# An attention and mixture-of-experts kernel: all float32 products of a tile in four 64x64 quadrants, the first expert's weights loaded from tile 12 on

## The chip, the cores and the metric

The kernel runs on one core of one Trainium2 chip. The metric is the device time in microseconds (us) of one execution, as a median of several runs. A core has TensorE (PE, with its weight loads, PEld, as a row of their own), VectorE (DVE), ScalarE (ACT), GpSimd (POOL) and the queue that issues most DMAs (SP). Line numbers (L239) are those of the kernel before, unless the text says otherwise.

## What is computed

Chunked attention, without a mask, over 4,608 tokens (8 batches of 576, in chunks of 64), and then a layer of experts on its output, in which each token goes to one expert or none:

```python
scores = scale * np.matmul(q_c, k_c.transpose(0, 1, 2, 4, 3))   # chunks of 64, D = 64
scores = scores - np.max(scores, axis=-1, keepdims=True)
attn = np.exp(scores)
attn = attn / (np.sum(attn, axis=-1, keepdims=True) + 1e-09)
x = np.matmul(attn, v_c)          # -> 4608 tokens of 512
...
skip_score = x @ w_skip           # only tokens with skip_score > 0 go on
logits = xc @ w_gate              # 8 experts
e_idx = np.argmax(logits, axis=1)
...
    h = np.maximum(xc[mask] @ w1[e], 0.0)          # 512 -> 1024
    y[mask] = gate_w[mask, None] * (h @ w2[e])     # 1024 -> 512
out[do_compute] = xc + y
```

## The kernel before

**Two parts.** The first part works on 36 tiles of 128 tokens (two chunks of 64, all 8 heads) in float32 and writes the attention's output to `out`. The second gathers the tokens of each expert in blocks of up to 128 rows and runs them through the two layers with float16 pairs (a high and a low part). Between the two, a routing step over groups of 4 to 6 tiles works out for each token its expert and its row.

**A tile's products on TensorE.** Five groups of matmuls belong to each tile, and each float32 matmul stands in the trace as two weight loads and two matmuls, each float32 transpose as one of each:
- `pe_scores` (L232 to L240): q times k, 16 products of 64x64 by 64x64, in four quadrants of the array (two halves of the rows, two of the columns), into a two-bank PSUM tile `sc`; 32 loads and 32 matmuls.
- `pe_ptrans` (L262): four transposes of 128x128 into one PSUM bank, of the pool `ps_s` with two buffers; 4 and 4. `ac_pt` (L269) copies the result to SBUF on ACT.
- `pe_pv` (L274): the attention times v, 16 products in quadrants, into `xq`, two banks; 32 and 32.
- `pe_logit` (L307): the product with `w_skip` and `w_gate`, four accumulating matmuls of 128x128 by 128x9, into spare columns of the `xq` of a later tile; 8 and 8. `ve_logit` (L315) copies the 9 columns out on DVE.
- `pe_xt` (L295): four transposes of 128x128 of the attention's output into the other `ps_s` buffer; 4 and 4. `ac_xt` (L302) copies it out on ACT.

Between them stand `ac_scores` (L242), `ve_max` (L247, the row maximum on DVE and the subtraction on POOL), `ac_exp` (L257) and `ve_x` (L285, the division on DVE, and the DMA of the tile to `out` on SP).

**The order is written out by hand.** The loop at L636 runs steps i = 0 to 41; step i issues the scores of tile i, the first transpose of tile i-2, the product with v of tile i-3, the logits of tile i-5 and the second transpose of tile i-4, in that order on TensorE. On each engine and on SP the work runs in the order in which the loop issues it. The q and k of a pair of tiles are loaded (L130) four pairs ahead, with five buffers; the v of a pair likewise. In the last six steps, in which no new tile begins, parts of the first expert's first layer (`l1_steps`, L487, with PSUM banks of `ps_s`) are put between (`DRAIN`).

**The first expert's weights.** `W_LOAD` lists the eight steps in which a pair of weight chunks of 512 KB is loaded (`load_pair`, L349, four buffers), `W_CONV` eight steps in which one of the sixteen halves is converted, the high part on ACT (L359) and the low part on DVE (L360). The eight halves that are left are converted after the loop (L760). In steps 32 and 38 POOL gathers the first blocks of the second part from `out` (`gather_at`, L652), ahead of the step's `ve_max` in POOL's order.

**PSUM** has eight banks here: `rk` one, `ps_s` two, `dbank` one, `sc` two, `xq` two. After the loop the first part's pools are closed and `bpool` and `ps_h` take their room (L691 to L694).

## Time and profile before

| | |
|---|---|
| median of three runs | 391.61 us (391.16 to 392.31) |
| the profiled execution | 391.34 us, of which the span from the first to the last instruction is 389.5 us |
| mean granted TensorE clock over the span | 0.944 |
| tile 0 to tile 33 begun on TensorE | 5.3 to 130.5 us |
| last logits of the first part | about 165 us |
| second part | from there to the end |

The profile gives busy time by engine, groups of instructions by line, a timeline by engine, the chain of waits that ended last, the DMA queues with their packets, and sums by stretches of time. In a timeline, what stands in square brackets at a row's end is the idle time of the engine ahead of it and what ended it; "issue" is time in which the engine waited for nothing that the profile shows. In the rows of stretches, x and a number is the count of instructions that began in the stretch.

### The profile page before, as it was taken

The page shows a single profiled execution, that of the slowest core. Times are in us where ns is not written, and L with a number is a line of the kernel's source. Part 1 is how long each engine was busy: PE and PEld are TensorE (multiplying, and loading weights), DVE is VectorE, ACT ScalarE, POOL GpSimd, SP SyncE. Part 2 cuts the span into 40 slices and gives each one's busy share as a digit, 9 for nine tenths or more (in the row PEclk, how much of TensorE's full clock was granted, in tenths as well). Part 3 has the DMA queues.
Part 4 walks back from the last instruction along what each step waited for, and adds up shares of the span by engine and source line. Part 5 has one row for each costly group of instructions (what it writes and reads, how often), then busy time and mean ns, then how long its engine had stood idle before and what let it go on. Part 6 is the DMA issues. An engine that isn't in the chain of part 4 may idle for free.

```text
span 389.5 us, 11031 instructions
## 1 busy us (share of the span) xinstructions
PE 359.6 (92%) x4472; PEld 256.1 (66%) x4472; DVE 248.3 (64%) x580; ACT 185.8 (48%) x319; POOL 125.5 (32%) x151
## 2 busy tenths in 40 slices
PE   6989899999999799867988999999999999999992
PEld 3667788888788588843575554475574766758470
DVE  2444447796577548477976776677696767966520
ACT  2665537676566454260152554455365444645220
POOL 4332217363353724212171411421513335111000
PEclk9899659999899979996998999999999999999998
DMA  7999979999862311200763676577756876655000
GB/s 262 415 404 412 408 282 306 332 337 371 313 248 82 111 56 56 82 0 0 259 197 134 215 237 232 164 262 223 255 183 187 276 230 217 206 186 183 27 24 26
DMA packets 26792, 81.81 MB, mean 210 GB/s; under 512 B 3335, under 2 KB 3336, under 8 KB 26738
## 3 DMA queue, kind: packets, MB, share of 16 engines
q1 hardware_dynamic: 23634, 71.74, 53.7%
q0 software_dynamic: 3104, 9.33, 6.5%
q8 instruction: 37, 0.61, 0.6%
q14 instruction: 17, 0.14, 0.1%
HBM read 67.20 MB, written 14.35 MB: 209 GB/s over the span
## 4 chain that ended last, share of the span: by engine, by line
PE 79%; DVE 6%; issue 6%; DMA 3%; POOL 2%; ACT 1%; SPq 0%; POOLq 0%; DVEq 0%
PE sp L516 23%; PE hp L494 19%; PE xq L312 9%; PE xq L282 6%; PE sc L239 6%; PE sp L266 5%; PE sp L299 4%; PE sp L494 2%; PE xt L479 2%; DMA xg<-out,recsi 2%; DVE wset L360 2%; DMA st<-in_qk 1%; PE rk L158 1%; PE rk L449 1%; DVE x L524 1%
## 5 line engine op out<-in xcount | busy, mean ns | idle before, releaser
L516 PE MATMUL sp<-wset,ht 128*128 128x512 f16 (+2 forms) x528 | 107.4, 387 | 0.0
L494 PEld LDWEIGHTS <-wset 128*128 128x128 f16 x864 | 79.8, 98 | 21.4 <-issue 3.1
L494 PE MATMUL hp<-xt,wset 128*128 128x288 f16 (+4 forms) x768 | 89.3, 278 | 0.9 <-DVE xt L481 0.6
L516 PEld LDWEIGHTS <-ht 128*128 128x128 f16 (+2 forms) x528 | 45.4, 100 | 50.4 <-issue 6.3
L216 DVE SCALAR_TENSOR_TENSOR wset<-wst,wset 128x1024 f16<-128x1024 f32 x56 | 67.6, 1217 | 9.5 <-ACT wset L215 9.5
L251 POOL TENSOR_TENSOR px<-sc,mx 128x512 f32<-128x512 f32 x36 | 39.0, 1085 | 87.2 <-DVE mx L249 85.8
L219 POOL DMA_INDIRECT out<-x,recsi x18 | 24.9, 1382 | 114.5 <-DVE x L524 99.3
L215 ACT ACTIVATE wset<-wst 128x1024 f16<-128x1024 f32 x56 | 57.7, 1048 | 0.0
L498 ACT ACTIVATE ht<-hp 128x288 f16<-128x288 f32 (+4 forms) x64 | 25.2, 393 | 61.1 <-PE hp L494 59.8
L499 DVE SCALAR_TENSOR_TENSOR ht<-hp,ht 128x288 f16<-128x288 f32 (+4 forms) x64 | 27.1, 433 | 23.4 <-ACT ht L498 22.7
L312 PE MATMUL xq<-csb,xc 128*128 128x9 f32 x288 | 41.0, 270 | 0.0
L312 PEld LDWEIGHTS xq<-csb,xc 128*128 128x128 f32 x288 | 37.9, 205 | 2.5
L288 DVE TENSOR_SCALAR rr<-xq 128x8 f32<-128x8 f32 x36 | 5.9, 164 | 49.2 <-PE xq L312 46.4
L480 ACT ACTIVATE xt<-xt 128x512 f16<-128x512 f32 (+2 forms) x20 | 10.6, 528 | 53.1 <-PE xt L479 39.8
L304 ACT ACTIVATE xc<-sp 128x512 f32<-128x512 f32 x36 | 21.4, 594 | 26.7 <-PE sp L299 26.7
L282 PE MATMUL xq<-sv,pz 64*64 64x65 f32 x1152 | 27.7, 234 | 4.1 <-issue 3.5
L239 PE MATMUL sc<-st 64*64 64x64 f32 x1152 | 28.3, 240 | 3.5 <-DMA st<-in_qk 2.2
L259 ACT ACTIVATE px<-px 128x512 f32<-128x512 f32 x36 | 22.6, 628 | 18.5 <-POOL px L251 18.5
L239 PEld LDWEIGHTS sc<-st 64*64 64x64 f32 x1152 | 22.8, 148 | 11.6 <-issue 9.4
L249 DVE TENSOR_REDUCE mx<-sc 128x8 f32<-128x512 f32 x36 | 24.4, 677 | 8.7 <-ACT sc L244 8.7
L282 PEld LDWEIGHTS xq<-sv,pz 64*64 64x64 f32 x1152 | 22.2, 143 | 11.7 <-issue 9.4
L266 PE MATMUL sp<-csb,px 128*128 128x128 f32 x144 | 25.9, 305 | 3.3 <-ACT px L259 2.9
(173 smaller groups left out, 389.0 us busy)
## 6 DMA issues: line engine op xcount, KB each, us to landing
wst<-in_wall SPq DMA_DIRECT2D x64, 512.0 KB, 4.4
st<-in_qk SPq DMA_DIRECT2D x34, 512.0 KB, 7.8
sv<-in_vo SPq DMA_DIRECT2D x18, 520.0 KB, 7.7
out<-xa SPq DMA_DIRECT2D x36, 256.0 KB, 3.5
st<-in_qk SPq DMA_DIRECT2D x4, 256.0 KB, 3.5
xg<-out,recsi POOLq DMA_INDIRECT x18, 5.7
out<-x,recsi POOLq DMA_INDIRECT x18, 5.1
csb<-in_cst SPq DMA_DIRECT2D x1, 266.5 KB, 4.6
```

Of the source, the lines that this page charges most:

```text
L215: nc.scalar.activation(w[:, 0, fc, :], st, AF.Copy, scale=SW)
L216: nc.vector.scalar_tensor_tensor(w[:, 1, fc, :], st, SW, w[:, 0, fc, :], op0=ALU.mult, op1=ALU.subtract)
L219: ins = nc.gpsimd.indirect_dma_start(**kw)
L239: nc.tensor.matmul(sp[halves[c], a, j], st[halves[r], 0, i, w], st[halves[r], 1, i, w], start=(j == 0), stop=True, skip_group_check=True)
L251: nc.gpsimd.tensor_tensor(px, T[t].pop("sc"), mx.unsqueeze(2).to_broadcast([P, H, CH]), op=ALU.subtract)
L266: nc.tensor.transpose(pt[:, j, :], px[:, j].rearrange("p a s -> p (a s)"), ident)
L282: nc.tensor.matmul(xq[w, a, j * (D + 1):(j + 1) * (D + 1)], pz[r, j, w], v[r, c, j], start=(j == 0), stop=True, skip_group_check=True)
L312: nc.tensor.matmul(lg, xc[:, j], C("wsg")[:, j * (NE + 1):(j + 1) * (NE + 1)], start=(j == 0), stop=(j == KC - 1), skip_group_check=True)
L494: nc.tensor.matmul(hp, w()[:, a, fc, j * P:(j + 1) * P], xt[:, b, j, :n], start=(m == 0), stop=(m == 11))
L498: nc.scalar.activation(ht[:, 0, fc, :n], hp, AF.Relu)
L499: nc.vector.scalar_tensor_tensor(ht[:, 1, fc, :n], hp, 0.0, ht[:, 0, fc, :n], op0=ALU.max, op1=ALU.subtract)
L516: nc.tensor.matmul(y[c * P // cg:c * P // cg + n], ht[:, a, fc, o:o + n], w[:, b, fc, P * KC:], start=(f == 0 and m == 0), stop=(f == fw - ...
```

## The change

1. Both transposes are made in quadrants: 16 float32 products of a 64x64 piece with a 64x64 identity in place of four transposes of 128x128, into one two-bank tile `tp`, which has a single buffer and serves both transposes. ACT copies it out from two banks.
2. The logits are 16 products of 64x64 by 64x9, into both banks of `xq`; DVE adds the two banks in place of the copy.
3. `ps_s`, the two-bank pool, is opened only after the tile loop's step 35; its room is that of `sc`, which goes into a pool of its own.
4. `W_LOAD` and `W_CONV` move to later steps.
5. In a step, the early gathers come after `ve_max` in place of ahead of it.
6. `bpool` and `ps_h` are given the option `reuse_waits="tile"`.

```diff
-W_LOAD = (3, 6, 10, 14, 17, 20, 22, 24)
-W_CONV = (7, 10, 12, 13, 15, 18, 19, 22)
+W_LOAD = (12, 14, 16, 18, 21, 25, 29, 33)
+W_CONV = (15, 17, 19, 21, 23, 25, 27, 29)
...
-    ps_s = ctx.enter_context(tc.tile_pool(name="ps_s", bufs=2, space=PSUM))
...
+    scpool = tc.tile_pool(name="ps_c", bufs=1, space=PSUM, side="right")
+    ps_c = scpool.__enter__()
...
+    QUADS = ((0, 0), (1, 1), (0, 1), (1, 0))
...
+    def two_banks(pool, name):
+        return pool.tile([P, 2, DM], F32, name=name)[:, :, :KC * CH].rearrange("p a (j s) -> p a j s", j=KC)
+
+    def by_quads(src):
+        dst = two_banks(ps_p, "tp")
+        for j in range(KC):
+            for r, c in QUADS:
+                nc.tensor.matmul(dst[halves[c], r, j], src[halves[r], j * P + c * CH:j * P + (c + 1) * CH], ident[halves[r], halves[r]], start=(j == 0), stop=True, skip_group_check=True)
+        return dst
+
+    def from_quads(dst, src):
+        nc.scalar.activation(dst.rearrange("p j (r q) -> p r j q", r=2), src, AF.Copy)
...
     def pe_ptrans(t):
-        px = T[t].pop("px")
-        pt = bank().rearrange("p (k q) -> p k q", k=KC)
-        for j in range(KC):
-            nc.tensor.transpose(pt[:, j, :], px[:, j].rearrange("p a s -> p (a s)"), ident)
-        T[t]["pt"] = pt
+        T[t]["pt"] = by_quads(T[t].pop("px"))
...
     def pe_xt(t):
-        x = T[t].pop("x")
-        xp = bank().rearrange("p (k q) -> p k q", k=KC)
-        for j in range(KC):
-            nc.tensor.transpose(xp[:, j, :], x[:, j * P:(j + 1) * P], ident)
-        T[t]["xp"] = xp
+        T[t]["xp"] = by_quads(T[t].pop("x"))
...
     def pe_logit(t):
...
-        lg = xq[:, 0, XW:XW + NE + 1]
+        lg = xq[:, :, XW:XW + NE + 1]
         for j in range(KC):
-            nc.tensor.matmul(lg, xc[:, j], C("wsg")[:, j * (NE + 1):(j + 1) * (NE + 1)], start=(j == 0), stop=(j == KC - 1), skip_group_check=True)
+            for r, c in QUADS:
+                nc.tensor.matmul(lg[halves[c], r], xc[halves[r], j, halves[c]], C("wsg")[halves[r], j * (NE + 1):(j + 1) * (NE + 1)], start=(j == 0), stop=(j == KC - 1), skip_group_check=True)
...
-        nc.vector.tensor_copy(lgs[g][:, i], T[t].pop("lg"))
+        nc.vector.tensor_reduce(lgs[g][:, i], T[t].pop("lg").rearrange("p a n -> p n a"), axis=AX.X, op=ALU.add)
...
-        for m in gather_at.get(i, ()):
-            early_gather(m)
         on(ve_x, i - 4)
         on(ve_logit, i - 6)
         on(ve_max, i - 1)
+        if i == NT:
+            scpool.__exit__(None, None, None)
+            ps_s = ctx.enter_context(tc.tile_pool(name="ps_s", bufs=2, space=PSUM, side="right"))
+        for m in gather_at.get(i, ()):
+            early_gather(m)
...
-    bpool = ctx.enter_context(tc.tile_pool(name="bpool", bufs=3))
-    ps_h = ctx.enter_context(tc.tile_pool(name="ps_h", bufs=3, space=PSUM))
+    bpool = ctx.enter_context(tc.tile_pool(name="bpool", bufs=3, reuse_waits="tile"))
+    ps_h = ctx.enter_context(tc.tile_pool(name="ps_h", bufs=3, space=PSUM, reuse_waits="tile"))
```

More of the change, by code (lines that the diff above doesn't have):

```diff
@@ L230, in fill @@
             budget -= c
+    def two_banks(pool, name):
[8 more added lines that the diff above has]
+        nc.scalar.activation(dst.rearrange("p j (r q) -> p r j q", r=2), src, AF.Copy)
     def pe_scores(t):
         st, i = T[t].pop("st"), t % TP
-        sp = ps_p.tile([P, 2, DM], F32, name="sc")[:, :, :KC * CH].rearrange("p a (j s) -> p a j s", j=KC)
+        sp = two_banks(ps_c, "sc")
         for j in range(KC):
-            for k in range(4):
-                a, r, c = k // 2, k % 2, (k + k // 2) % 2
+            for r, c in QUADS:
+                a = r ^ c
                 w = slice((2 * j + a) * CH, (2 * j + a + 1) * CH)
@@ L259, in ac_exp @@
         nc.scalar.activation(px, px, AF.Exp, scale=1.0 / math.sqrt(D))
-        T[t]["px"] = px.rearrange("p (j a) s -> p j a s", a=2)
+        T[t]["px"] = px.rearrange("p h s -> p (h s)")
     def pe_ptrans(t):
-        px = T[t].pop("px")
-        pt = bank().rearrange("p (k q) -> p k q", k=KC)
-        for j in range(KC):
-            nc.tensor.transpose(pt[:, j, :], px[:, j].rearrange("p a s -> p (a s)"), ident)
-        T[t]["pt"] = pt
+        T[t]["pt"] = by_quads(T[t].pop("px"))
     def ac_pt(t):
         pz = ap.tile([P, KC, P], F32, name="pz", bufs=2)
-        nc.scalar.activation(pz, T[t].pop("pt"), AF.Copy)
+        from_quads(pz, T[t].pop("pt"))
         T[t]["pz"] = pz
@@ L278, in pe_pv @@
         for j in range(KC):
-            for k in range(4):
-                a, c = k % 2, (k + k // 2) % 2
+            for a, c in QUADS:
                 r, w = halves[a], halves[c]
@@ L295, in pe_xt @@
     def pe_xt(t):
-        x = T[t].pop("x")
-        xp = bank().rearrange("p (k q) -> p k q", k=KC)
-        for j in range(KC):
-            nc.tensor.transpose(xp[:, j, :], x[:, j * P:(j + 1) * P], ident)
-        T[t]["xp"] = xp
+        T[t]["xp"] = by_quads(T[t].pop("x"))
     def ac_xt(t):
         xc = ap.tile([P, KC, P], F32, name="xc", bufs=2)
-        nc.scalar.activation(xc, T[t].pop("xp"), AF.Copy)
+        from_quads(xc, T[t].pop("xp"))
         T[t]["xc"] = xc
@@ L309, in pe_logit @@
         xq = T[t + 2]["xq"] if t + 2 < NT else ps_p.tile([P, 2, DM], F32, name="xq")
-        lg = xq[:, 0, XW:XW + NE + 1]
+        lg = xq[:, :, XW:XW + NE + 1]
         for j in range(KC):
-            nc.tensor.matmul(lg, xc[:, j], C("wsg")[:, j * (NE + 1):(j + 1) * (NE + 1)], start=(j == 0), stop=(j == KC - 1), skip_group_check=True)
+            for r, c in QUADS:
+                nc.tensor.matmul(lg[halves[c], r], xc[halves[r], j, halves[c]], C("wsg")[halves[r], j * (NE + 1):(j + 1) * (NE + 1)], start=(j == 0), stop=(j == KC - 1), skip_group_check=True)
         T[t]["lg"] = lg
```

## The prediction

> **What bounds the kernel now.** I read the page's head, then the first part in stretches, then TensorE's timeline in a quiet tile and in a disturbed one, then the DMA packets around the disturbed ones. The page says how many instructions TensorE gets, and that a DMA queue of its own carries instructions:

> ```profile
> span 389.5 us, 11031 instructions
> PE 359.6 (92%) x4472; PEld 256.1 (66%) x4472; DVE 248.3 (64%) x580; ACT 185.8 (48%) x319; POOL 125.5 (32%) x151
> ...
> q8 instruction: 37, 0.61, 0.6%
> L239 PE MATMUL sc<-st 64*64 64x64 f32 x1152 | 28.3, 240 | 3.5 <-DMA st<-in_qk 2.2 <-issue 1.3
> L266 PE MATMUL sp<-csb,px 128*128 128x128 f32 x144 | 25.9, 305 | 3.3 <-ACT px L259 2.9 <-issue 0.3
> L312 PE MATMUL xq<-csb,xc 128*128 128x9 f32 x288 | 41.0, 270 | 0.0
> ```

> 0.61 MB in 37 packets is 16 KB each. The groups are from the view of lines with shapes kept apart: over 36 tiles, 1152 is 32 matmuls per tile for the scores, 144 is 4 for a transpose, 288 is 8 for the logits. The first part in stretches (columns: length; busy us and instructions of PE, PEld, DVE, ACT, POOL; granted clock; DMA share; GB/s):

> ```profile
> 8.20:23.00 14.80, 13.77 (x305) 9.57 (x305) 6.86 (x19) 9.08 (x16) 4.53 (x5) 0.88 1.03 413
> 23.00:42.50 19.50, 16.24 (x385) 13.64 (x385) 7.89 (x22) 12.34 (x21) 5.58 (x5) 1.00 1.03 408
> 42.50:59.50 17.00, 17.00 (x227) 14.31 (x231) 8.63 (x27) 6.59 (x13) 3.37 (x4) 0.50 0.87 329
> 59.50:97.10 37.60, 37.32 (x898) 32.17 (x891) 28.01 (x87) 26.79 (x50) 18.99 (x30) 1.00 0.95 337
> 97.10:131.20 34.10, 32.94 (x744) 27.96 (x743) 23.91 (x88) 19.93 (x36) 14.85 (x28) 0.95 0.53 196
> 131.20:165.40 34.20, 29.86 (x448) 25.86 (x449) 18.70 (x74) 14.84 (x29) 13.79 (x27) 0.90 0.24 79
> ```

> TensorE is busy nearly throughout, except at 23 to 42.5, where the DMA engines are full. A quiet tile, then TensorE's disturbed places:

> ```profile
> 61.45 0.69 PE L239 MATMUL sc<-st 64*64 64x64 f32 x32
> 62.07 0.66 PE L266 MATMUL sp<-csb,px 128*128 128x128 f32 x4
> 62.66 0.70 PE L282 MATMUL xq<-sv,pz 64*64 64x65 f32 x32
> 63.28 1.06 PE L312 MATMUL xq<-csb,xc 128*128 128x9 f32 x8
> 64.20 0.64 PE L299 MATMUL sp<-csb,xa 128*128 128x128 f32 x4
> 64.76 0.69 PE L239 MATMUL sc<-st 64*64 64x64 f32 x32
> ```

> ```profile
> 21.98 0.34 PE L239 MATMUL sc<-st 64*64 64x64 f32 x6
> 23.03 0.68 PE L239 MATMUL sc<-st 64*64 64x64 f32 x26 [0.72 <-issue]
> ...
> 29.39 0.46 PE L282 MATMUL xq<-sv,pz 64*64 64x65 f32 x16 [1.38 <-issue]
> ...
> 35.68 0.45 PE L239 MATMUL sc<-st 64*64 64x64 f32 x14 [0.55 <-issue]
> ...
> 41.95 0.33 PE L282 MATMUL xq<-sv,pz 64*64 64x65 f32 x4 [1.29 <-issue]
> ...
> 99.09 0.62 PE L282 MATMUL xq<-sv,pz 64*64 64x65 f32 x26 [0.85 <-issue]
> ```

> A quiet tile takes 64.76 - 61.45 = 3.31 us, with no gap: 0.62, 0.59, 0.62, 0.92, 0.56 us from start to start. The disturbed places are the finding. TensorE stops in the middle of a group (after 6 of 32 matmuls), where no data can be missing, and four of these stops end 6.3 us apart. What came between two stops, and what the instruction queue q8 did meanwhile (stretches 23.02 to 29.37 and 29.37 to 35.67; packets of 23.02 to 26.9, 26.9 to 27.0, 103.3 to 103.5 and 106.6 to 106.7):

> ```profile
> 23.02:29.37 6.35, 4.97 (x126) 4.12 (x126) 2.10 (x6) 3.97 (x7) 2.08 (x2) 1.00 1.03 403
> 29.37:35.67 6.30, 5.75 (x126) 4.90 (x127) 3.73 (x11) 3.71 (x7) 1.42 (x1) 1.00 1.03 408
> ```

> ```profile
> q1 hardware_dynamic: 515, 1.57, 102.2%
> ```

> ```profile
> q8 instruction: 1, 0.02, 67.1%
> ```

> ```profile
> q8 instruction: 1, 0.02, 30.1%
> ```

> ```profile
> q8 instruction: 1, 0.02, 55.5%
> ```

> **The change part by part.** *Quadrants in place of transposes and logits.* By durations alone this is a gain. At each change between 128x128 and 64x64 TensorE's loads sit idle:

> ```profile
> 24.22 0.56 PEld L282 LDWEIGHTS xq<-sv,pz 64*64 64x64 f32 x32 [0.17 <-issue]
> ```

> A group of 32 that needs no change of shape should thus take 0.62 - 0.17 = 0.45 us, and five of them 2.25 us in place of 3.31. [...]

> By count it is a loss. Per tile the transposes go from 4 + 4 to 32 + 32 (loads and matmuls), twice, and the logits from 8 + 8 to 32 + 32: 56 + 56 + 48 = 160 more instructions, 320 per tile in place of 160. In 2.25 us that asks for a block each 1.8 us, and none came faster than 3.3. So I expect TensorE to wait for instructions throughout the tile loop, and cost the stretch from 23.0 us to 131.2 (scores of tiles 6 to 33) in blocks. Instructions now, from the rows of stretches: 770 + 458 + 1789 + 1487 = 4504. Added: 27 tiles by 160 = 4320, and 384 that the first tiles add ahead of 23.0 (four and two transposes and one logits group by 56 and 48), which must be fetched too. Together 9208, or 36.0 blocks of 256.

> The price of a block is the unknown. Below: 3.3 us, the shortest seen; 36.0 x 3.3 = 119 us. Above: 6.3 us with full queues; 227 us, but that can't last, since the stretch's 32.9 MB (the rows' lengths by their GB/s) are 80 us of transfers at 412 GB/s, and a slower tile loop leaves the queues emptier. Taking the price as a straight line from 3.3 at a low DMA share to 6.3 at 1.03, the share being 80 us over the stretch, gives 4.7 us and 169 us. I take less, because transfers come in bursts: those of one step (0.26 MB out, and 0.5 or 1 MB in) last 2 to 3 us, and a request that falls into one waits for the rest of it, some 1.2 us, in 58% of cases (80 us over 140). 3.3 + 0.7 = 4.0 us, and 36.0 x 4.0 = 144 us against 108.2 now: +36, with ends of +11 and +61. Nothing hides this: TensorE is the engine that the chain runs through.

> A lower granted clock, as in the row of 0.50, would cost little on top. A group of 32 takes 1.06 us there (the chain of waits):

> ```profile
> 44.81 1.06 PE sc L239 x32
> ```

> Five of them are 5.3 us at most, about the 320/256 x 4.0 = 5.0 us that fetching a tile takes. I count it in the upper end.

> *One buffer `tp` for both transposes.* A transpose now waits until ACT has copied the one before it. In the quiet tile the copy ends 0.77 us after the group behind the transposes began:

> ```profile
> 64.93 0.60 ACT L304 ACTIVATE xc<-sp 128x512 f32<-128x512 f32 x1
> ```

> Behind the first transpose stand two groups, which cover it; behind the second only the scores, 0.45 us, so 0.77 - 0.45 = 0.32 us per tile is left: a tile of 2.25 + 0.32 = 2.6 us, if instructions came. Queued behind the waiting matmul are the product with v and all that follows. Under 5 us of fetching it is covered: zero.

> *Weights later.* The same bytes; three loads of 0.5 MB leave the full stretch before 42.5, others come after; on SP each still stands behind its step's loads of q, k and v and ahead of the tile's output. As tiles are fetch-bound, each load makes some block later wherever it stands: 0, within 4 us either way. The conversions on ACT and DVE lie beside TensorE, and eight halves are left for the end, as now (a group of the lines, and the chain):

> ```profile
> L359 ACT ACTIVATE wset<-wst 128x512 f16<-128x512 f32 x16 | 9.5, 619 | 0.6 <-DMA wst<-in_wall 0.6
> ```

> ```profile
> 177.79 4.90 DVE wset L360 x8
> ```

> *Gathers behind the subtraction.* Now a gather holds POOL ahead of a step's subtraction, which TensorE waits for (the chain of waits):

> ```profile
> 131.26 1.01 POOL xg L219
> ...
> 132.30 1.06 POOL px L251
> ...
> 134.06 0.66 PE sp L266 x4
> ```

> With the order turned round the subtraction goes first; that saves 1 to 3 us of the wait before 134.06, and the gather comes a microsecond later; its reader, the block's transposes, stands two steps on.

> *The last steps.* From 131.2 to 165.4 are 897 instructions; 1056 of the added 5760 are left for it: 1953, 7.6 blocks, at 3.3 us 25 us. That is under the 34.2 us that this stretch takes, which is a chain of waits across engines. So: -3 from the gathers, within -6 and +6, since fetches and waits may add up.

> *The rest* (the reduction on DVE in place of a copy, `reuse_waits`, the pool's later opening) lies beside TensorE: zero, within 2 us either way. The second part's instructions don't change, and fetching doesn't bind there, with 2348 of them in 174 us, a block in 19 us:

> ```profile
> 215.00:389.00 174.00, 166.66 (x1175) 103.93 (x1173) 114.34 (x158) 77.33 (x121) 47.33 (x34) 0.99 0.58 187
> ```

> Sum, on the profiled execution's 391.3 us (span 389.5 and 1.8 around it; the median of the runs is 391.6, the same within 0.1%): 391.3 + 36 - 3 = 424 us. With the ends: 391.3 + 11 - 6 = 396, and 391.3 + 61 + 6 = 458.

> **The rivals.** *Faster: instructions keep up.* If a second block can be on its way while TensorE asks for more, or blocks come faster than 3.3 us when asked faster, the tile falls to the 2.6 us of the buffer `tp`: 27 tiles by 0.7 is -19 (the 80 us of transfers still fit into the 89 that are left), the gathers -3, 369 us. For it: before, in quiet stretches, nobody needed a block sooner than each 5 us, so the least price is never measured under hunger and empty queues at once. Against it: four stops 6.3 us apart, with no packet begun in the 3.9 us after the restart. [...]

> *No change: the price falls to 3.0 us.* At 108.2 / 36.0 = 3.0 us per block the stretch is as long as now. Of that, 2.5 us pass between packet and restart anyway (26.9 to 29.39). Then 391.3 - 3 = 388, or 391 with some loss at the end. It needs the request to reach an idle DMA engine nearly always; with the DMA engines busy for 80 of 108 us that is unlikely.

> *Slower for another reason:* instructions keep up, but the single `tp` and ACT's three copies and one exponential (2.4 us at 0.6 each), with conversions in between, hold a tile above 3.31 us. The point is a copy that ends 0.7 us later than I count; a conversion of 0.62 us ahead of it nearly gets there, in eight tiles: 8 by 0.6 is +5 against the -19. That ends at 374 us and goes with the first rival.

> **How the numbers follow.** Forecast, fetch-bound tile loop, 396 to 458 us: 0.75. Instructions keep up, 365 to 386 us: 0.20. Price near 3.0 us, 386 to 396 us: 0.05. A difference of 0.3%, about 1.2 us, is what a measurement can tell from none. Of the third case nearly all lies outside of that, on both sides. Faster by over 0.3%: 0.22; within 0.3%: 0.03; slower: 0.75. The predicted time is 424. The range takes the forecast's case but for its last tenth (up to 455) and reaches down to 378, which takes in the case near 3.0 and some of the first rival's. The forecast's own range is 396 to 458.

> **What would show it.** Right: some 58 to 60 packets on q8 in place of 37, and 4472 + 2880 = 7352 matmuls; in the tile loop, stops that end on "issue" in the middle of groups, every 256 instructions, 3.3 to 5 us apart; tiles of 4 to 6 us. Groups of 32 at 0.47 us between stops would show the gain from unchanged shapes as real but unused. Wrong: packets on q8 closer than 3 us together, tiles under 3.3 us, TensorE's waits ending on ACT's copy (the single `tp`). Then the first rival holds, and my reading that one block at a time is on its way is the step that failed.

## The result, and the profile after

| | before | after |
|---|---|---|
| median of four runs on one chip | 391.96 us (391.16 to 395.23) | 446.53 us (443.38 to 449.66) |
| the profiled execution | 391.34 us | 447.94 us |
| its span | 389.5 us | 446.1 us |
| mean granted clock | 0.944 | 0.854 |

The ratio is 1.137 (95% interval 1.127 to 1.148): slower, by 55 us. Executions that ran over 1.5% longer than the fastest of their kernel are left out of the ratios here and below, so a ratio need not be that of the medians. The page of after (from its head, slices, queues, the shares of the chain of waits, and the groups):

```profile
span 446.1 us, 16738 instructions
PE 367.9 (82%) x7352; PEld 273.5 (61%) x7352; DVE 250.2 (56%) x580; ACT 185.7 (42%) x319; POOL 125.0 (28%) x151
...
q8 instruction: 59, 0.97, 0.9%
...
PE 73%; issue 16%; DVE 4%; DMA 3%; ACT 1%; POOL 1%; SPq 0%; POOLq 0%; ACTq 0%; DVEq 0%
...
L254 PE MATMUL sc<-st 64*64 64x64 f32 x1152 | 37.0, 269 | 15.4 <-issue 12.9
L241 PE MATMUL tp<-csb,px 64*64 64x64 f32 x1152 | 36.4, 274 | 15.7 <-issue 12.8
```

7352 matmuls and 59 packets of instructions, 22 more than before. TensorE's busy time rose by only 8 us for 64% more matmuls. The time is in the last column: 12.9 and 12.8 us of idle time ahead of the scores and the first transpose end on "issue", and "issue" holds 16% of the chain that ended last, where it held 6% before.

Where the 56.6 us of the two profiled executions come from is read by cutting both at the same events: the scores of tile 6 begun, of tile 33 begun, and the last logits done. Stretches of before, then of after (columns as in the prediction):

```profile
22.00:130.50 108.50, 103.12 (x2214) 87.70 (x2213) 68.75 (x222) 66.25 (x119) 42.33 (x66) 0.91 0.83 307
130.50:165.10 34.60, 30.25 (x479) 26.13 (x479) 19.07 (x74) 14.84 (x29) 14.25 (x28) 0.90 0.24 78
165.10:389.50 224.40, 208.06 (x1444) 130.94 (x1443) 152.69 (x265) 94.11 (x153) 60.67 (x43) 0.97 0.53 170
```

```profile
31.60:190.60 159.00, 113.00 (x4379) 104.95 (x4376) 70.60 (x223) 66.30 (x120) 43.91 (x68) 0.69 0.56 188
190.60:224.00 33.40, 27.40 (x1021) 23.84 (x1013) 19.07 (x72) 14.69 (x28) 12.01 (x26) 0.91 0.25 82
224.00:446.10 222.10, 206.02 (x1453) 130.07 (x1448) 152.67 (x265) 94.11 (x154) 60.80 (x44) 0.98 0.53 172
```

Tiles 6 to 33 take 50.5 us more, the tiles ahead of them 9.6 (31.6 against 22.0), the last steps 1.2 less and the second part 2.3 less; together 56.6. In the long stretch TensorE is busy for 113 of 159 us, where it was for 103 of 108.5, and the DMA engines are emptier, not fuller (0.56 against 0.83). So of the 50.5 us 9.9 are more busy time, at a lower clock, and 40.6 more idle time; by the view of waits 44.1 us of TensorE's idle time there end on "issue", where 4.8 did before. In this stretch the view of the DMA queues lists

```profile
q8 instruction: 34, 0.56, 1.4%
```

so 159.0 / 34 = 4.68 us per block, and 4379 + 4376 = 8755 records are 34.2 blocks of 256. TensorE's timeline shows how a block is lived on:

```profile
81.91 1.01 PE L241 MATMUL tp<-csb,px 64*64 64x64 f32 x25
84.30 0.38 PE L241 MATMUL tp<-csb,px 64*64 64x64 f32 x4 [1.38 <-issue]
...
87.06 0.94 PE L254 MATMUL sc<-st 64*64 64x64 f32 x24
89.40 0.38 PE L254 MATMUL sc<-st 64*64 64x64 f32 x4 [1.40 <-issue]
```

It stops inside a group, once in the first transpose and 5.1 us later in the scores, and each stop is 1.4 us long. Stretches that are cut by turns at a restart of TensorE and at the start of the next q8 packet (78.94 restart, 81.89 packet, 84.30 restart, and so on; a count takes in every instruction that runs in a row, so that one at a border stands in both):

```profile
78.94:81.89 2.95, 2.95 (x103) 2.87 (x102) 1.56 (x5) 1.09 (x2) 1.32 (x8) 0.50 0.90 329
81.89:84.30 2.41, 1.03 (x29) 0.93 (x26) 1.30 (x3) 0.60 (x1) 2.16 (x2) 0.50 0.55 144
84.30:87.20 2.90, 2.90 (x109) 2.90 (x112) 0.66 (x3) 1.12 (x2) 0.65 (x1) 0.50 0.84 336
87.20:89.40 2.20, 0.81 (x31) 0.62 (x24) 1.08 (x3) 0.60 (x1) 1.04 (x1) 0.50 0.50 153
89.40:93.28 3.88, 3.70 (x128) 3.51 (x127) 0.78 (x3) 2.23 (x4) 0.00 (x0) 0.50 0.75 263
93.28:95.50 2.22, 0.00 (x0) 0.00 (x0) 1.55 (x4) 0.00 (x0) 1.19 (x1) 0.50 0.54 137
```

Odd rows run from restart to packet (2.95, 2.90, 3.88 us), even rows from packet to restart (2.41, 2.20, 2.22). The DMA share is 0.75 to 0.90 in the odd rows and 0.50 to 0.55 in the even ones. Each even row holds a stop: TensorE is busy in it for 1.03, 0.81 and 0.00 us. The long stretch is like these rows for the most part: 27 of its 34 packets are followed by a stop of 0.2 us or more, which ends 2.2 to 2.7 us behind the packet's start, 2.37 on average. The other seven blocks came before TensorE had used up the one ahead of them. Between the ends of two stops stand 254 to 256 loads and matmuls, or 510 where one block without a stop lies between. From a restart to the next packet 1.0 to 3.9 us pass, 2.3 on average, at a DMA share of 0.74; from there to the restart the share is 0.43. So I read that one block at most is on its way, and that it is asked for when the one ahead of it has come.

### The profile page after: what moved, and what is told of

The parts are those of the page before. It is cut to its first block, busy times and chain, and to the rows that moved or that the text cites. A ratio compares the mean times of both kernels' runs of the same rounds, so it can differ in the third digit from the quotient of the medians.

```text
span 446.1 us, 16738 instructions
## 1 busy us (share of the span) xinstructions
PE 367.9 (82%) x7352; PEld 273.5 (61%) x7352; DVE 250.2 (56%) x580; ACT 185.7 (42%) x319; POOL 125.0 (28%) x151
## 4 chain that ended last, share of the span: by engine, by line
PE 73%; issue 16%; DVE 4%; DMA 3%; ACT 1%; POOL 1%; SPq 0%; POOLq 0%; ACTq 0%; DVEq 0%
PE sp L523 20%; PE hp L501 16%; PE tp L241 14%; PE xq L292 6%; PE sc L254 5%; PE xq L319 5%; PE sp L501 2%; PE xt L486 2%; DMA xg<-out,recsi 2%; DMA st<-in_qk 1%; ACT xc L245 1%; DVE wset L367 1%; PE rk L456 1%; PE rk L160 1%; DVE x L531 1%
## 5 line engine op out<-in xcount | busy, mean ns | idle before, releaser
L266 POOL TENSOR_TENSOR px<-sc,mx 128x512 f32<-128x512 f32 x36 | 39.0, 1085 | 146.2 <-DVE mx L264 144.0
L254 PE MATMUL sc<-st 64*64 64x64 f32 x1152 | 37.0, 269 | 15.4 <-issue 12.9
L241 PE MATMUL tp<-csb,px 64*64 64x64 f32 x1152 | 36.4, 274 | 15.7 <-issue 12.8
L245 ACT ACTIVATE xc<-tp 128x512 f32<-128x512 f32 x36 | 21.5, 597 | 65.7 <-PE tp L241 65.7
L241 PE MATMUL tp<-csb,xa 64*64 64x64 f32 x1152 | 37.4, 269 | 9.4 <-issue 9.4
L254 PEld LDWEIGHTS sc<-st 64*64 64x64 f32 x1152 | 32.5, 180 | 18.6 <-issue 18.1
L292 PE MATMUL xq<-sv,pz 64*64 64x65 f32 x1152 | 36.9, 270 | 8.3 <-issue 8.3
L319 PE MATMUL xq<-csb,xc 64*64 64x9 f32 x1152 | 33.3, 222 | 10.8 <-issue 10.7
L241 PEld LDWEIGHTS tp<-csb,px 64*64 64x64 f32 x1152 | 29.8, 179 | 19.8 <-issue 14.3
L319 PEld LDWEIGHTS xq<-csb,xc 64*64 64x64 f32 x1152 | 31.9, 177 | 11.9 <-issue 11.8
L292 PEld LDWEIGHTS xq<-sv,pz 64*64 64x64 f32 x1152 | 31.8, 181 | 11.2 <-issue 10.4
L241 PEld LDWEIGHTS tp<-csb,xa 64*64 64x64 f32 x1152 | 31.9, 178 | 10.5 <-issue 10.5
```

Source lines behind the costliest of these rows:

```text
L241: nc.tensor.matmul(dst[halves[c], r, j], src[halves[r], j * P + c * CH:j * P + (c + 1) * CH], ident[halves[r], halves[r]], start=(j == 0), ...
L245: nc.scalar.activation(dst.rearrange("p j (r q) -> p r j q", r=2), src, AF.Copy)
L254: nc.tensor.matmul(sp[halves[c], a, j], st[halves[r], 0, i, w], st[halves[r], 1, i, w], start=(j == 0), stop=True, skip_group_check=True)
L266: nc.gpsimd.tensor_tensor(px, T[t].pop("sc"), mx.unsqueeze(2).to_broadcast([P, H, CH]), op=ALU.subtract)
L292: nc.tensor.matmul(xq[w, a, j * (D + 1):(j + 1) * (D + 1)], pz[r, j, w], v[r, c, j], start=(j == 0), stop=True, skip_group_check=True)
L319: nc.tensor.matmul(lg[halves[c], r], xc[halves[r], j, halves[c]], C("wsg")[halves[r], j * (NE + 1):(j + 1) * (NE + 1)], start=(j == 0), st ...
```

## The experiments

The theory, which I call the fetch theory: the tile loop is bound by the delivery of TensorE's instructions, one block of 256 at a time, and the price of a block depends on what the DMA engines do while it is awaited. Its rivals: the lower clock (0.69 in the long stretch) is what costs the time; the single `tp` makes TensorE wait for ACT; the later weights do. The runs stand beside runs of the kernel before on the same chip, whose medians were 390.67, 389.27 and 391.79 us for the three groups of runs below. In the tables "long stretch" is from the scores of tile 6 to those of tile 33, and packets are those of q8 in it.

### The added instructions, taken back in three steps

`n160` is after with both transposes of 128x128 again, into the first bank of the same single `tp`, and the logits as before; its count of instructions per tile is that of before. In `n208` only the logits stay in quadrants, in `n264` the logits and the first transpose. The edit, for one transpose:

```diff
-        T[t]["xp"] = by_quads(T[t].pop("x"))
+        x = T[t].pop("x")
+        xp = ps_p.tile([P, 2, DM], F32, name="tp")[:, 0].rearrange("p (k q) -> p k q", k=KC)
+        for j in range(KC):
+            nc.tensor.transpose(xp[:, j, :], x[:, j * P:(j + 1) * P], ident)
+        T[t]["xp"] = xp
```

> The changed kernel with both transposes and the logits back in 128x128 (160 instructions per tile on TensorE as before), all else of the change kept: the single buffer tp, the later weights, the gathers behind the subtraction, the option of the later pools. Fetch theory (a block of 256 instructions costs TensorE 4.5 to 4.7 us and the count sets the tile loop): 18 blocks in the stretch of tiles 6 to 33, no more than TensorE's own 3.3 us per tile, so 384 to 396 us in all. Rival, the single tp and ACT's copies hold a tile: the tile loop stays near 5 us per tile, 430 us or more. Rival, the late weight loads cost the time: 430 us or more as well.

> As the one with 160, but the logits stay in quadrants: 208 instructions per tile. Fetch theory: some 23 blocks of 4.5 us, 104 us for the stretch that took 108 before: 385 to 405 us in all, with stops that end on issue in every tile. By durations alone (no fetch bound) it would gain about 0.4 us per tile on the one with 160, 12 us or more. Rival single tp: 430 us or more.

> The changed kernel with only the second transpose back in 128x128: 264 instructions per tile. Fetch theory: some 29.6 blocks of 4.6 us, 136 us for the stretch: 405 to 425 us, on a line with the kernels of 208 and 320 by count. By durations alone it would be slower than the changed kernel, since it brings back two changes of shape per tile. Rival clock (the granted clock of one half in most of the tile loop is the cause, not the fetching): no line by count; 440 us or more as long as the clock stays at one half.

| | instructions per tile | median, us | long stretch, us | packets in it | clock in it | second part, us |
|---|---|---|---|---|---|---|
| before | 160 | 390.67 | 108.5 | 18 | 0.91 | 224.4 |
| `n160` | 160 | 387.98 (381.89 to 390.8) | 110.4 | 18 | 0.92 | 222.4 |
| `n208` | 208 | 399.41 (395.73 to 400.74) | 122.1 | 23 | 0.82 | 222.1 |
| `n264` | 264 | 419.96 (415.7 to 421.99) | 135.3 | 28 | 0.77 | 222.6 |
| after | 320 | 446.53 | 159.0 | 34 | 0.69 | 222.1 |

(The row of before has its median from this chip, and the rest from the profiled execution shown above; the row of after is from the first comparison.) The ratios are 1.027 (1.012 to 1.041) for `n208` and 1.074 (1.057 to 1.090) for `n264`. The long stretch of the three, in this order:

```profile
22.00:132.40 110.40, 103.52 (x2213) 86.93 (x2212) 70.36 (x223) 67.71 (x120) 42.75 (x67) 0.92 0.82 297
```

```profile
23.80:145.90 122.10, 102.74 (x2865) 84.91 (x2864) 70.06 (x222) 66.85 (x120) 45.08 (x69) 0.82 0.76 270
```

```profile
29.80:165.10 135.30, 106.72 (x3618) 93.91 (x3617) 68.47 (x217) 67.33 (x120) 42.06 (x66) 0.77 0.66 221
```

TensorE's busy time stays between 103 and 107 us, while its records go from 4425 to 7235. The length follows the records, which the count of packets mirrors: 122.1 / 23 = 5.3 us per block at a DMA share of 0.76, 135.3 / 28 = 4.8 at 0.66, 159.0 / 34 = 4.7 at 0.56. A stop stands behind 13 of the 23 packets, 18 of the 28 and 27 of the 34; so in `n208` 5.3 us is the distance of the blocks, and TensorE needed part of it for its own work. All three totals lie in the expected ranges, but `n208` by the width of its range: 4.5 us a block and 104 us for the stretch were expected. With the instructions back at 160 per tile, all of the loss is gone, though the single `tp`, the later weights and the turned gathers are still there. Up to here the lower clock goes along with the loss and is not told apart from it.

### The transfers taken away

`light` is after without the loads of q, k and v from the fifth pair of tiles on; those tiles compute on the data of the first four pairs. With such data the scores and so the choice of experts are others, and the second part takes 494 us in place of 222 with more matmuls than after has (8162 in all against 7352), so its total of 690.43 us is not comparable; its tile loop is.

```diff
+    st_keep = [T[u * TP]["st"] for u in range(AHEAD)]
+    sv_keep = [T[u * TP]["sv"] for u in range(AHEAD)]
...
         if i % TP == 1 and u + AHEAD < NU:
-            st_load(u + AHEAD, (0, 1))
-        if i % TP == 0 and i and u - 1 + AHEAD < NU:
-            st_load(u - 1 + AHEAD, (2,))
+            for a in (0, 1):
+                T[(u + AHEAD) * TP + a]["st"] = st_keep[u % AHEAD]
+                T[(u + AHEAD) * TP + a]["sv"] = sv_keep[u % AHEAD]
```

> The changed kernel without the loads of q, k and v from the fifth pair of tiles on: those tiles compute on the first four pairs' data, so the results are those of other inputs; TensorE's 320 instructions per tile are the same. Fetch theory: with the DMA engines mostly idle a block costs 3.4 to 3.6 us, 126 us for the stretch of tiles 6 to 33 in place of 167: 400 to 415 us in all. Rival clock or single tp: nothing changes for TensorE, 440 to 450 us.

```profile
26.70:161.50 134.80, 96.35 (x4385) 88.11 (x4378) 70.38 (x222) 65.21 (x120) 44.78 (x69) 0.85 0.28 89
```

The same instructions in 134.8 us in place of 159.0, at half the DMA share. Their 8763 records are 34.2 blocks, of 3.94 us each, where the same count gives 4.65 in after. From restart to packet it takes 1.5 us on average (1.2 in the median, at a DMA share of 0.40) in place of 2.3 (2.4); from packet to restart 2.45, the same as with the loads. So 24 us of the loss go with the transfers, and lie ahead of the packet. The expected 3.4 to 3.6 us a block and 126 us were missed: the outputs and weights still run, and some waits are long (up to 3.3 us). Even here TensorE is busy for only 96 of 135 us. The clock is also higher, 0.85, which `light` alone doesn't tell from the fetches.

### The clock by itself

`warm` is after with two products of 128x512 in float16, of zeros, ahead of each transposing group, into the same banks, to lift the clock.

```diff
-        dst = two_banks(ps_p, "tp")
+        full = ps_p.tile([P, 2, DM], F32, name="tp")
+        dst = full[:, :, :KC * CH].rearrange("p a (j s) -> p a j s", j=KC)
+        for a in range(2):
+            nc.tensor.matmul(full[:, a], ones, zeros, start=True, stop=True, skip_group_check=True)
         for j in range(KC):
             for r, c in QUADS:
```

> The changed kernel with two dense float16 products of 128x512 ahead of each transposing group, written into tp and overwritten by it: 8 more instructions per tile, about 1 us more of TensorE's own work and two more changes of shape. They should hold the granted clock up (0.69 on average in the stretch of tiles 6 to 33 of the changed kernel). Fetch theory: the extra work falls into the waits for instructions, the count rises by 2.5%: 444 to 458 us in all, whatever the clock does. Rival clock (half speed sets the tile): with the clock at 0.85 or more the tile loop shortens by 20 us or more, 425 us or less.

```profile
33.06:200.74 167.68, 127.14 (x4489) 93.23 (x4488) 70.39 (x223) 65.96 (x120) 46.14 (x69) 0.87 0.54 178
```

The row is the long stretch. The clock is 0.87 in place of 0.69, and nothing is won: one run took 458.27 us, just above what was expected, the long stretch 167.7 us, a block 4.79 us. The added products have 8 more records per tile (2 for each product, two groups), 2.5% more to fetch. TensorE is idle for 40.5 us of the stretch, and 36.9 of them end on "issue". So the low clock is not what sets the time of the tile loop: the 20 us that this rival needed are not there. The added products are work too, so this one run cannot show that the clock is worth nothing at all.

### The single `tp`, and a better version

`two160` is `n160` with `tp` as two buffers of one bank. `order160` is `two160` with both transposes next to each other in TensorE's order, behind the logits, so that the shape changes twice per tile less. The edits, the first for one of the two transposes:

```diff
-        pt = ps_p.tile([P, 2, DM], F32, name="tp")[:, 0].rearrange("p (k q) -> p k q", k=KC)
+        pt = ps_p.tile([P, DM], F32, name="tp", bufs=2).rearrange("p (k q) -> p k q", k=KC)
```

```diff
-        on(pe_ptrans, i - 2)
-        on(ac_pt, i - 2)
         on(ac_exp, i - 1)
...
         on(pe_pv, i - 3)
         on(pe_logit, i - 5)
+        on(pe_ptrans, i - 2)
+        on(ac_pt, i - 2)
         on(pe_xt, i - 4)
```

> The kernel with 160 instructions per tile and the later weights and gathers, with two buffers of one bank for the transposes in place of the single one: 0.1 to 0.2 us less waiting per tile if the single buffer held it. 382 to 390 us, 0 to 5 us under the kernel with the single buffer. Fetch theory: the gain shows only in tiles that don't wait for a block.

> As the one before, with TensorE's order in a step scores, product with v, logits, first transpose, second transpose: two changes between 64x64 and 128x128 per tile in place of four, with the same instructions. By durations 2 x 0.15 us per tile, 8 us over the tiles 6 to 33. Fetch theory: 160 instructions in 3.0 us ask for a block each 4.8 us, no more than one costs with the DMA engines half full, so half of the gain or less: 380 to 387 us. If blocks came as fast as asked: 375 to 380 us.

`two160` takes 383.06 us (379.68 to 384.16), a ratio to before of 0.985 (0.979 to 0.991): 1.5% shorter than before, and far shorter than after. Of the 10.0 us between the profiled executions (391.34 and 381.36, of separate comparisons), 3.4 lie in the long stretch (22.0 to 127.1, 105.1 us), 4.7 in the last steps (127.1 to 157.0, 29.9 us) and 1.8 in the second part (222.6 us).

The second buffer's share can be read within a quiet tile. The scores and the first transpose in `n160`, then in `two160`:

```profile
68.13 0.69 PE L254 MATMUL sc<-st 64*64 64x64 f32 x32
68.95 0.65 PE L281 MATMUL tp<-csb,px 128*128 128x128 f32 x4
```

```profile
67.10 0.69 PE L254 MATMUL sc<-st 64*64 64x64 f32 x32
67.73 0.66 PE L281 MATMUL tp<-csb,px 128*128 128x128 f32 x4
```

With the single buffer the transpose begins 0.82 us after the scores, with two 0.63, as before. 0.19 us over 27 tiles are 5.1 us, and the long stretches of the two differ by 5.3 (110.4 and 105.1). The view of waits does not list a wait this short.

`order160` takes 384.43 us, ratio 0.987 (0.981 to 0.993), so no better. Its quiet tile is shorter, but in the long stretch five stops end on "issue", 6.6 us in all, where `two160` has four with 3.2 us. TensorE's timeline of `order160`:

```profile
29.21 0.45 PE L296 MATMUL xq<-sv,pz 64*64 64x65 f32 x11 [2.08 <-issue]
...
53.64 0.60 PE L281 MATMUL tp<-csb,px 128*128 128x128 f32 x4 [1.30 <-issue]
...
70.43 0.69 PE L254 MATMUL sc<-st 64*64 64x64 f32 x32
70.95 0.68 PE L296 MATMUL xq<-sv,pz 64*64 64x65 f32 x32
71.55 1.06 PE L326 MATMUL xq<-csb,xc 128*128 128x9 f32 x8
72.47 0.64 PE L281 MATMUL tp<-csb,px 128*128 128x128 f32 x4
72.94 0.60 PE L313 MATMUL tp<-csb,xa 128*128 128x128 f32 x4
73.47 0.69 PE L254 MATMUL sc<-st 64*64 64x64 f32 x32
...
96.58 0.45 PE L296 MATMUL xq<-sv,pz 64*64 64x65 f32 x12 [1.20 <-issue]
```

The long stretch of `two160`, then that of `order160`:

```profile
22.00:127.10 105.10, 100.02 (x2212) 85.06 (x2206) 69.57 (x222) 66.93 (x120) 43.05 (x67) 0.94 0.87 314
```

```profile
22.00:129.30 107.30, 99.46 (x2212) 89.43 (x2208) 69.44 (x223) 64.48 (x121) 42.56 (x67) 0.89 0.85 308
```

A quiet tile of 73.47 - 70.43 = 3.04 us, against 3.3, meets the next block's arrival sooner: with 160 instructions per tile, 256 last for 1.6 tiles, 4.9 us in place of 5.3. The 3.4 us of added stops fit the same limit already at 160 instructions per tile. But they are less than half of the 8 us that the shorter tiles promise. The clock differs too: 0.11 of 107.3 us are 12 us of full clock missing, 0.06 of 105.1 are 6, by my estimate. So the cause is not isolated, and the clock may be the larger part.

### The smaller parts

`wearly` is after with the lists `W_LOAD` and `W_CONV` of before; `latew` is before with those of after; `gather` is before with the early gathers behind `ve_max`; `reuse` is before with the option `reuse_waits="tile"` on the two pools.

```diff
-W_LOAD = (12, 14, 16, 18, 21, 25, 29, 33)
-W_CONV = (15, 17, 19, 21, 23, 25, 27, 29)
+W_LOAD = (3, 6, 10, 14, 17, 20, 22, 24)
+W_CONV = (7, 10, 12, 13, 15, 18, 19, 22)
```

```diff
-        for m in gather_at.get(i, ()):
-            early_gather(m)
         on(ve_x, i - 4)
         on(ve_logit, i - 6)
         on(ve_max, i - 1)
+        for m in gather_at.get(i, ()):
+            early_gather(m)
```

```diff
-    bpool = ctx.enter_context(tc.tile_pool(name="bpool", bufs=3))
-    ps_h = ctx.enter_context(tc.tile_pool(name="ps_h", bufs=3, space=PSUM))
+    bpool = ctx.enter_context(tc.tile_pool(name="bpool", bufs=3, reuse_waits="tile"))
+    ps_h = ctx.enter_context(tc.tile_pool(name="ps_h", bufs=3, space=PSUM, reuse_waits="tile"))
```

> The changed kernel with the weights' loads and conversions back in their old steps, from tile 3 on: the same bytes and instructions. Fetch theory: each load makes some block later, wherever it stands, so within 4 us of the changed kernel, 442 to 451 us. Rival: the late loads make the tile loop slow; then 435 us or less. If the early stretch with full queues matters more than the later one: 450 us or more.

> The kernel before with only the weights' loads and conversions in the later steps. Forecast's term: 0, within 4 us. Fetch theory: early stops on issue get fewer or shorter (three loads of 0.5 MB less before 42 us), and there are as many more later: 387 to 393 us.

> The kernel before with only the early gathers behind the subtraction. The forecast's term: 1 to 3 us of the wait ahead of tile 32's first transpose go, 388 to 391 us; the stretch from tile 33's scores to the last logits shortens from 34.6 us by as much. Rival: another wait in that stretch takes its place, 391 us. Nothing here touches the fetching: 37 instruction packets.

> The kernel before with only the option reuse_waits on the two later pools. All kernels with the whole rest of the change ran from the last logits to the end in 221 to 223 us, the kernel before in 224.4. If the option is the cause, 222 to 223 us here; if not, 224 to 225 us. The tile loop stays as before.

`wearly` takes 446.68 us (442.71 to 448.83), as after does (446.53); its blocks cost 4.60 us. `latew` has a ratio of 1.000 (0.991 to 1.008). So the place of the weights is worth nothing that these runs can tell, with either form of the products.

`gather` has a ratio of 0.982 (0.965 to 0.999), a wide interval, since this chip's runs of before spread from 383.82 to 397.82 us: 0.4 to 13 us, where 1 to 3 were expected. Its profile shows where: the wait that the prediction named, in TensorE's timeline of before,

```profile
134.06 0.66 PE L266 MATMUL sp<-csb,px 128*128 128x128 f32 x4 [2.87 <-ACT px L259]
```

is gone from that step, and one of 1.0 us is left a step later; in `gather`:

```profile
135.60 0.65 PE L266 MATMUL sp<-csb,px 128*128 128x128 f32 x4
...
140.43 0.66 PE L266 MATMUL sp<-csb,px 128*128 128x128 f32 x4 [1.00 <-ACT px L259]
```

The last steps take 30.9 us in it (135.0 to 165.9), 3.7 less than before's 34.6, at a clock of 0.94 against 0.90. `latew` and `reuse`, with the gathers of before, take 37.2 and 38.1 us there, at 0.82 and 0.78. So part of these differences may be the clock.

`reuse` took 393.62 us in one run. Its second part is 222.1 us long against 224.4, as was expected if the option is the cause. But of the two other kernels that lack the option, the second part of `latew` takes 222.9 and that of `gather` 224.5. So the 2 us which the second part of after is shorter are not put down to the option; their cause stays open.

## Why the prediction came out as it did

The direction, the mechanism and the range were right; one term, the price of a block, was too small.

**Instructions in blocks, one at a time: right.** The counts came as worked out (7352 matmuls; 59 packets for 58 to 60), and in the long stretch TensorE stops for 27 of 34 blocks. The ladder of `n208`, `n264` and after ties the loss to the count of instructions, and `n160` shows that nothing else of the change costs anything near it. The rival by which a second block is on its way, and the one by which the price falls to 3.0 us, are out: the packets were 4.68 us apart, and even `light`, with half of the transfers, paid 3.94 us a block. No two packets in the long stretch of either came closer than 3.36 us. The size of a block is in the traces: each of the 59 packets of after has 16,384 bytes, and in before 126 loads, 126 matmuls and 4 semaphore instructions of TensorE lie between the restarts at 23.02 and 29.37, 256 in all, so 64 bytes each.

**The price of a block: the step that was mis-sized.** I took 4.0 us and 144 us from 23.0 us to tile 33; the trace of after has 190.6 - 23.0 = 167.6 us. The straight line through 3.3 us at a low DMA share and 6.3 at full queues had given 4.7 us and 169 us, and I replaced it by an argument about chance, an estimate of mine: a request meets a burst in 58% of cases (80 over 140 is 57) and waits for 1.2 us. The rows show more than that: the mean wait from restart to packet is 2.3 us, where 0.7 above a floor of 0.8 (3.3 less 2.5) makes 1.5. The floor was low, since the smallest waits are 1.0 to 1.1 us, and with the 2.4 that follow they make 3.5 us a block. And the waits above the floor were not much more frequent than I had put them, but longer: of the 29 that can be told in the long stretch of after, 19 (66%) are of 1.95 us or more, 2.9 on average, which is 1.8 above the floor and not 1.2. Why they are longer is not shown. The DMA share is 0.74 from a restart to the next packet and 0.43 from there to the restart; that would fit a request that stands near the start of a burst more often than at a random place in it, but no run isolates it. The 23.6 us between 144 and 167.6 are nearly the whole miss: 424 and 23.6 are 447.6, and the profiled execution took 447.9. The two smaller misses, 1.8 us more in the last steps and 2.3 less in the second part, cancel.

The straight line that I dropped holds for the other kernels as well. With the measured GB/s of the long stretch over 412 as the share, 3.3 + 3.0 x share gives 3.95 us for `light`, 4.67 for after, 4.91 for `n264` and 5.27 for `n208`; by their records, 256 to a block, the blocks took 3.94, 4.65, 4.79 and 5.46.

**The clock: nearly right.** I counted nothing for it in the forecast. `warm` bears that out for the tile loop, as far as one run can. The row of 78.94 to 81.89 shows it in small: 205 records in 2.95 us at half clock, all of them ahead of the packet; at the 0.44 to 0.49 us that a group of 32 takes at a clock of 1.00 (below), these 103 matmuls would have taken some 1.5 us, by my estimate, and the stop would have been longer by the rest.

**Unchanged shapes: real, and unused.** Between stops, at a granted clock of 1.00 (128.97 to 132.72), TensorE's timeline of after reads

```profile
128.97 0.60 PE L319 MATMUL xq<-csb,xc 64*64 64x9 f32 x32
129.41 0.67 PE L241 MATMUL tp<-csb,xa 64*64 64x64 f32 x32
129.90 0.65 PE L254 MATMUL sc<-st 64*64 64x64 f32 x32
130.86 0.34 PE L241 MATMUL tp<-csb,px 64*64 64x64 f32 x7 [0.31 <-ACT xc L245]
132.72 0.58 PE L241 MATMUL tp<-csb,px 64*64 64x64 f32 x25 [1.53 <-issue]
```

Groups of 32 follow each other in 0.44 and 0.49 us, as worked out (0.45), where they took 0.56 to 0.92 before; then the instructions are out. The logits, 0.92 us as eight wide products, take 0.44. By duration the change does what the shapes promise. In the quiet tile of before the loads of each group of 64x64 that follows one of 128x128 start behind 0.17 us of idle time (61.45, 62.66 and 64.76), those of the other groups behind 0.1 or less; in after the loads of these rows at 128.97, 129.41 and 129.90 follow each other without an idle time that the timeline lists.

**The single `tp`: right.** The fourth of these rows has the wait that I had expected: 0.31 us for ACT's copy of the other transpose (0.32 in the prediction). The view of waits, for the long stretch of after (us in total, times, longest):

```profile
PE tp L241 <- issue: 19.3, 13, 3.6
PE sc L254 <- issue: 12.4, 6, 3.2
...
PE tp L241 <- ACT xc L245: 2.0, 7, 0.3
```

It comes 7 times and costs 2.0 us where the stops of these two lines alone are 31.7. With 160 instructions per tile it shows more, 0.19 us in a quiet tile of `n160`, since there is less fetching to cover it.

**Gathers and last steps: right in sign, less than half in size.** I took 3 us off; after has 1.2 less, `gather` alone 3.7. In after the last steps hold 2034 records, 7.9 blocks, and run at a DMA share of 0.25; at the 3.94 us that `light` paid at 0.28 they would be 31 of the 33.4 us. I had set them at 25 us of fetching under a chain of 34.2. So fetching and the chain are nearly equal there. In after 3.8 us of stops end on "issue" in the last steps, in before and in `n160` none, and `n160`, with the gathers of after, takes 31.2 us. So the added instructions are likely what ate the rest of the gathers' gain; but the clock there is 1.00 in `n160` and 0.91 in after, and no run keeps the two apart.

**The rest: near its bounds.** Weights at zero (`wearly`, `latew`), the second part 2.3 us shorter where I had 0 within 2 either way, so just outside them, its cause open.

## What to carry to other kernels

Count TensorE's instructions as a resource beside its busy time: here a float32 matmul is four of them (the 16 products of the scores are 32 loads and 32 matmuls in the trace), and a block of 256 cost 3.9 us at a DMA share of 0.28, 4.7 at 0.56 and 6.3 at 1.03. By these prices I estimate that a stage of this kernel that asks for more than some 40 to 65 instructions per us stops (256 over 6.3 and over 3.9), whatever the durations of its matmuls say; where in that range depends on the load (before ran 48 per us from 59.5 to 97.1 us at a share of 0.95 with 0.3 us of idle time). The signs are in the profile before any change: stops inside a group that end on "issue" (four in before, 6.3 us apart), and packets on the instruction queue at about the same distance (26.95, 33.10 and 39.52 us). For a forecast, take the price from the rows' straight line, 3.3 + 3.0 x share (before has 3.3 us between the packets at 103.40 and 106.68, with a share of 0.12 at 105.80 to 106.65 ahead of the second, and 6.3 us at 1.03); it came within 0.2 us a block in four kernels. An argument about chance needs the length of a wait as much as its frequency, and here the length was what failed.

## What the runs showed of the hardware that was not expected

- From the start of a block's packet to the end of the stop behind it 2.2 to 2.7 us pass, with little regard to the load on the DMA engines (mean 2.37 us in after, 2.45 in `light`); the load goes with the time before the packet starts (1.0 to 3.9 us in after, 2.3 on average; 1.5 in `light`).
- TensorE does not always get the full clock when it has no gap: the row of 84.30 to 87.20 is busy for all of its 2.90 us at a granted clock of 0.50. Two dense products of 128x512 per transposing group brought the long stretch from 0.69 to 0.87, with 36.9 us of stops still in it. What the low clock is due to, no run shows.
- A shorter tile without fewer instructions brought nothing: `order160` made the quiet tile 0.3 us shorter, and the total stayed, with 3.4 us more of stops and a lower clock (0.89 against 0.94).
